# A second matrix product by Strassen's rule, in token blocks of 256

## The chip, the cores and the metric

The kernel runs on one core of a Trainium2 chip. Its engines work side by side, each through its own list of instructions in order: TensorE (matrix products; its weight loads are listed apart as PEld), VectorE (DVE), ScalarE (ACT), GpSimd (POOL), and SyncE (SP), which starts most of the DMA transfers. The metric is the device time of one execution in microseconds.

## What is computed

An attention block with a decaying state, followed by a feed-forward block. Cut to what matters:

```python
# q, k, v, f_logit: (4, 8, 768, 48)
f = 1 / (1 + exp(-f_logit))
for t in range(S):
    state = f[:, :, t, :, None] * state + einsum('bhd,bhe->bhde', k[:, :, t], v[:, :, t])
    y[:, :, t] = einsum('bhd,bhde->bhe', q[:, :, t], state)
x = y.transpose(0, 2, 1, 3).reshape(3072, 384)

h = x @ w_in                       # (3072, 384) @ (384, 2048)
g = h * erf(softplus(h))
out = g @ w_out                    # (3072, 2048) @ (2048, 384)
```

The kernel does the recurrence in 24 chunks of 128 tokens by matrix products, and the rest in blocks of several chunks. The weights come as 64-bit numbers and are turned into fp32 on the chip ("rounding"), in 16 pieces. The function of h is put together from a sigmoid and four tanh passes on ScalarE, and products on VectorE. All of it is fp32.

## The kernel before

A block has 3 chunks, so 384 tokens (TB), and there are 8 blocks. Each block passes through four stages: the chunk stages d, t, s and y, which end in the transposed x of the block; the first product (`hidden`); the activation; the second product (`project`). Stages of different blocks are interleaved on TensorE by a hand-made schedule: a loop goes through products one by one ("slots"), and at fixed slots it puts in chunk stages, steps of the activation and steps of the rounding.

The chunk stages, cut:

```python
def stage_d(g):
    ...
    nc.tensor.matmul(ps, lhsT=tri[:], rhs=lts[blk][:, j, :], start=True, stop=True)
    nc.scalar.activation(out=dp[:, :, 0:D], in_=ps..., func=AF.Exp, scale=-1.0)
    nc.scalar.activation(out=kd, in_=ps..., func=AF.Exp)
    ...
    nc.vector.tensor_tensor(out=qd[:, :, 0:D], in0=qns[g % NQ]..., in1=dp[:, :, 0:D], op=ALU.mult)
    (nc.vector if blk == 0 else nc.gpsimd).tensor_tensor(
        out=kd, in0=kns[g % NQ]..., in1=kd, op=ALU.mult)

def stage_t(g):          # four transposes of qd, four of kd, copied out as qT and kT
    ...
def stage_s(g):          # scores sc, A = sc * tri on VectorE, state: dS, Sn, Mbd (GpSimd)
    ...
def stage_y(g):          # y from A, v, qT and Mbd, copied to xT by ScalarE
    ...
```

The activation of one group of four tiles of d_ff (`h` is 128 x 1536). Each `yield` ends a step; a new group starts when the one before it has made LEAD = 5 steps:

```python
def activate(gr):
    h = gr["h"][:].rearrange("p j t -> p (j t)")
    e = epool.tile([P, FG * TB], FP32, name="e", tag="e")
    sigmoid(e, h)                          # ScalarE
    yield
    for i in range(n + 2):                 # n = 3
        if i < n:
            xs[i] = xpool.tile([P, FG * TB], FP32, name="x", tag="x")
            term(xs[i], h, i)              # ScalarE: tanh
        if i >= 2:
            times(e, xs.pop(i - 2), i - 2) # VectorE: e = (x + c) * e
        yield
    ...
    nc.scalar.activation(out=e[:], in_=e[:], func=AF.Tanh, scale=SERF_C)
    ...
    nc.vector.tensor_tensor(out=h, in0=h, in1=e[:], op=ALU.mult)
```

First and second product:

```python
def hidden(blk, gi):
    ...
    for u in range(FG // 2):
        hps = ps_moe.tile([P, 2, 512], FP32, name="hps", tag="moe")
        for j in range(2):
            ft = gi * FG + 2 * u + j
            for kt in range(n_k):                      # n_k = 3
                nc.tensor.matmul(
                    hps[:, j, 0:TB],
                    lhsT=w_in_sb[:, kt, ft * P : (ft + 1) * P],
                    rhs=xTs[blk][:, kt, :],
                    start=(kt == 0), stop=(kt == n_k - 1),
                )
                if j == 1 and kt == n_k - 1:
                    to = gr["h"][:, 2 * u : 2 * u + 2, :]
                    if blk < 2:
                        nc.scalar.copy(out=to, in_=hps[:, :, 0:TB])
                    else:
                        nc.vector.tensor_copy(out=to, in_=hps[:, :, 0:TB])
                    ...
                yield

def project(blk):
    ops = [ps_moe.tile([P, 2, 512], FP32, name="ops", tag="moe") ...]
    for gi in range(n_g):                              # n_g = 4
        for tt in range(CPB):                          # CPB = 3
            for j in range(FG):                        # FG = 4
                ft = gi * FG + j
                nc.tensor.matmul(
                    ops[tt // 2][:, tt % 2, 0:d_model],
                    lhsT=gr["h"][:, j, tt * P : (tt + 1) * P],
                    rhs=w_out_sb[:, ft, :],
                    start=(ft == 0), stop=(ft == n_ft - 1),
                )
                if ft == n_ft - 1 and tt == 1:
                    nc.scalar.copy(out=osb2[:], in_=ops[0][:, :, 0:d_model])
                    nc.sync.dma_start(...)             # 256 rows of the output
                if ft == n_ft - 1 and tt == 2:
                    nc.scalar.copy(out=osb1[:], in_=ops[1][:, 0, 0:d_model])
                    nc.sync.dma_start(...)             # 128 rows
                yield
```

The order of the loop: first product of block `it`, with the second product of block `it - 2` in its middle; chunk stages of block `it + 1`.

Of the kernel before, what the change touches and what calls it, by code (L numbers as in the profile page):

```python
# [65 lines left out]
P = 128  # L67
# [3 lines left out]
def kernel(  # L71
# [21 lines left out]
    CPB = 3  # L93
# [75 lines left out]
    epool = main.enter_context(tc.tile_pool(name="epool", bufs=3))  # L169
# [5 lines left out]
    NV, NQ, NG = 3, 3, 10  # L175
# [8 lines left out]
    Hgs = [fixed(f"Hg{i}", [P, FG, TB], pool=fix) for i in range(NG)]  # L184
    osb2 = fixed("osb2", [P, 2, d_model], pool=fix)
    osb1 = fixed("osb1", [P, d_model], pool=fix)
# [32 lines left out]
    HOMES = [("w", 0), ("w", 1), ("w", 2), ("w", 3), 4, 5, 6, 3] + [4, 5, 6, ("w", 2), ("w", 3), 7, 8, 9]  # L219
    ORDER = list(range(8)) + [8 + j for j in (0, 3, 1, 4, 2, 5, 6, 7)]  # L220

    def raw_home(i):
        if isinstance(HOMES[i], int):
            return Hgs[HOMES[i]][:].rearrange("p a t -> p (a t)")
        m = 2 * n_ft // n_pieces
        return w_out_sb[:, bass.ts(HOMES[i][1], m), :].rearrange("p a t -> p (a t)")
# [63 lines left out]

    xTs, As, qTs, kTs = {}, {}, {}, {}
# [35 lines left out]
    def stage_d(g):  # L327
        blk, j = divmod(g, CPB)
        if blk == 0:
            both = ps_moe.tile([P, 2, 512], FP32, name="ps_d0", tag="moe")  # L330
            ps, totals[g] = both[:, 0, 0:d_model], both[:, 1, 0:HP]
            busy.append(both[:, 1, P : 2 * P])
        else:
            ps = ps_at.tile([P, 512], FP32, name="ps_d", tag="at")[:, 0:d_model]
# [8 lines left out]
        if blk > 0:  # L343
            for a in range(HP):
                nc.sync.dma_start(
                    out=Tall[:, g, a : a + 1],
                    in_=dp[P - 1 : P, 2 * a : 2 * a + 2, :].rearrange("o r d -> o (r d)"),
                )
# [4 lines left out]
        (nc.vector if blk == 0 else nc.gpsimd).tensor_tensor(  # L353
# [3 lines left out]
    def stage_t(g):  # L357
        pss = []
        for src in (qd, kds[g % 2]):
            ps = ps_at.tile([P, HP, P], FP32, name="ps_t", tag="at")  # L360
            flat = src[:].rearrange("t (a r) d -> t a (r d)", r=2)
            for a in range(HP):
                nc.tensor.transpose(ps[:, a, :], flat[:, a, :], ident[:])  # L363
            pss.append(ps)
            if 0 < g < CPB and src is qd:
                keep_busy(3)
# [3 lines left out]
        if g < 3 * CPB:  # L370
# [58 lines left out]
    def stage_y(g):  # L429
# [4 lines left out]
        if blk == 0:  # L434
            keep_busy(3)
# [7 lines left out]
    def activate(gr):  # L443


        h = gr["h"][:].rearrange("p j t -> p (j t)")
# [23 lines left out]
    LEAD = len(SERF_KAB) + 2  # L470
# [12 lines left out]
    n_made = [0]  # L483

    def hidden(blk, gi):

        own = n_made[0] % NG
        gr = {"h": Hgs[own], "done": False}
        n_made[0] += 1
        groups[blk, gi] = gr  # L490
        for u in range(FG // 2):
            hps = ps_moe.tile([P, 2, 512], FP32, name="hps", tag="moe")
            for j in range(2):
                ft = gi * FG + 2 * u + j
                assert ft * n_pieces // n_ft in rounded
                for kt in range(n_k):
                    nc.tensor.matmul(  # L497
                        hps[:, j, 0:TB],
                        lhsT=w_in_sb[:, kt, ft * P : (ft + 1) * P],
                        rhs=xTs[blk][:, kt, :],  # L500
                        start=(kt == 0), stop=(kt == n_k - 1),
                    )
                    if j == 1 and kt == n_k - 1:
                        assert all(i in rounded for i, x in enumerate(HOMES) if x == own)
                        to = gr["h"][:, 2 * u : 2 * u + 2, :]
                        if blk < 2:
                            nc.scalar.copy(out=to, in_=hps[:, :, 0:TB])
                        else:
                            nc.vector.tensor_copy(out=to, in_=hps[:, :, 0:TB])  # L509
                        if u == FG // 2 - 1:  # L510
                            acts.append(activate(gr))
                    yield

    def project(blk):

        ops = [ps_moe.tile([P, 2, 512], FP32, name="ops", tag="moe")
               for _ in range(2 if blk < n_blocks - 1 else 1)]
        if blk == n_blocks - 1:

            ops.insert(0, ps_sc.tile([P, 2, 512], FP32, name="ops", tag="sc"))  # L520
        r = blk * TB
        for gi in range(n_g):
            gr = groups[blk, gi]
            for tt in range(CPB):
                for j in range(FG):
                    ft = gi * FG + j
                    assert n_pieces + ft * n_pieces // n_ft in rounded
                    while not gr["done"]:
                        act_step()
                    nc.tensor.matmul(  # L530
                        ops[tt // 2][:, tt % 2, 0:d_model],
# [4 lines left out]
                    if ft == n_ft - 1 and tt == 1:  # L536
                        nc.scalar.copy(out=osb2[:], in_=ops[0][:, :, 0:d_model])  # L537
                        nc.sync.dma_start(
                            out=out[r : r + 2 * P, :].rearrange("(t p) c -> p t c", p=P), in_=osb2[:]
                        )  # L540
                    if ft == n_ft - 1 and tt == 2:
                        nc.scalar.copy(out=osb1[:], in_=ops[1][:, 0, 0:d_model])
                        nc.sync.dma_start(out=out[r + 2 * P : r + TB, :], in_=osb1[:])
                    yield
# [4 lines left out]

    def slots(it):  # L550

        if it >= n_blocks:
            return project(it - 2)
        made = [hidden(it, gi) for gi in range(n_g)]
        return chain(*made) if it < 2 else chain(*made[:2], project(it - 2), *made[2:])

    n_h, n_o = n_ft * n_k, n_ft * CPB
    n_slots = [n_h] * 2 + [n_h + n_o] * (n_blocks - 2) + [n_o] * 2
# [17 lines left out]
    with tc.manual_schedule():  # L576
# [13 lines left out]
        for g in range(CPB, 2 * CPB):  # L590
            load_f(g)
# [62 lines left out]
        prepare(0, 2, 3)  # L654
# [15 lines left out]
        prepare(1, 0, CPB)  # L670
# [11 lines left out]
        def stages(blk):  # L682
            g0 = blk * CPB
            todo = []
            if blk == 1:
                todo = [(stage_d, g0), (stage_t, g0)]
            for g in range(g0, g0 + CPB):
# [9 lines left out]
        for it in range(n_blocks + 2):  # L697
            blk = it + 1
            if it + 2 < n_blocks:
                for j in range(CPB):  # L700
                    load_f((it + 2) * CPB + j)
            todo = deque(stages(blk) if blk < n_blocks else [])
            n = n_slots[it]
            at = [int(3 + (n - 13) / max(1, len(todo)) * i) for i in range(len(todo))]
            for s, _ in enumerate(slots(it)):
                due += 1 if it == 0 and s < 36 else 0.75
# [5 lines left out]
                if at and s == at[0]:  # L712
                    at.pop(0)
# [4 lines left out]
                if it + 2 < n_blocks and s == (16 if it < 2 else 30):  # L718
                    prepare(it + 2, 0, CPB)
                if it == 0:  # L720
                    step = s >= 16 and s % 8 == 4
                elif it == 1:
                    step = s % 8 == 4
                elif it == 2:
                    step = s % 3 == 1
                elif it < n_blocks:
                    step = s % 4 == 2
                else:
                    step = s % 3 == 2
                if step and not 66 <= s < 72:  # L730
                    act_step()
                if it == n_blocks - 1 and s in (5, 40):
# [216 lines left out]
```

## Time and profile before

| | |
|---|---|
| time, median of 3 | 647.7 us (647.5 to 647.84) |
| span of the profiled execution | 646.0 us |
| granted TensorE clock | 0.999 |
| ScalarE busy | 405.9 us (63%) |
| VectorE passes of the activation | 96 of 1806 ns, 32 of 1777 ns (mean) |
| GpSimd busy | 59.9 us (9%) |
| last product ends, last store is issued | 640.5 us, 641.1 us |

A line of the costliest groups reads: line of the kernel, engine, operation, what it writes and reads, shape, count, then busy time in us and the mean ns of one instruction, then the engine's idle time just before them and what ended most of it. A line of the timeline gives start and length in us of a run of equal instructions. A line of a table by stretch gives the stretch, its length, then busy us and count for TensorE, its weight loads, VectorE, ScalarE, GpSimd, then the granted clock, the DMA share and GB/s.

### The profile page before, as it was taken

What the parts mean: (1) busy time and instruction counts of PE and PEld (TensorE: products, weight loads), DVE (VectorE), ACT (ScalarE), POOL (GpSimd) and SP (SyncE); (2) the same over time, 40 slices, a digit from 0 to 9 for tenths busy, and PEclk for the clock granted to TensorE, in tenths of its full rate; (3) what the DMA queues carried; (4) which work ended last, traced back from release to release, by engine and by line L of the source; (5) the groups of instructions that cost most, each with busy time, mean ns of one, the idle gap of its engine ahead of it and who ended that gap; (6) DMA issues with size and microseconds to landing.
All of it is one profiled execution on the core that took longest, in us unless ns stands there. A gap on an engine that the chain in (4) does not pass through costs nothing.

```text
span 646.0 us, 9238 instructions
## 1 busy us (share of the span) xinstructions
PE 630.3 (98%) x3815; PEld 394.4 (61%) x3815; DVE 421.5 (65%) x408; ACT 405.9 (63%) x383; POOL 59.9 (9%) x61
## 2 busy tenths in 40 slices
PE   8999998999999999999999999999999999999996
PEld 7755665656666666666666566666666655555553
DVE  4798998899947765658654677447653686379100
ACT  5446768697888668656775757677564755276100
POOL 0112101111010000202210001100130000000000
PEclk9999999999999999999999999999999999999999
DMA  9995952310114120221202211020000000000101
GB/s 194 248 273 146 271 155 49 66 34 14 25 42 81 26 38 13 62 50 26 38 14 66 44 38 24 13 74 1 2 0 26 13 0 1 37 1 0 38 2 40
DMA packets 120688, 36.89 MB, mean 57 GB/s; under 512 B 112448, under 2 KB 115520, under 8 KB 120640
## 3 DMA queue, kind: packets, MB, share of 16 engines
q1 hardware_dynamic: 118560, 35.84, 24.1%
q10 hardware_dynamic: 2080, 0.39, 0.4%
q8 instruction: 32, 0.52, 0.3%
q14 instruction: 16, 0.13, 0.1%
HBM read 31.46 MB, written 4.72 MB: 56 GB/s over the span
## 4 chain that ended last, share of the span: by engine, by line
PE 89%; DVE 4%; ACT 3%; issue 2%; DMA 1%; SPq 0%; POOL 0%; ACTq 0%; POOLq 0%
PE ops L530 39%; PE hps L497 33%; PE y L145 5%; PE sc L381 3%; PE ps_t L363 3%; PE ps_d L335 2%; PE dS L409 1%; DVE e L159 1%; DVE w_out_sb L274 1%; PE ps_d L325 1%; PE busy L325 1%; DMA Tall<-dp 1%; PE ps_d L389 0%; DVE Hg L283 0%; ACT L299 0%
## 5 line engine op out<-in xcount | busy, mean ns | idle before, releaser
L497 PE MATMUL hps<-xT,w_in_sb 128*128 128x384 f32 x768 | 259.7, 489 | 1.1 <-ACT xT L438 0.6
L530 PE MATMUL ops<-w_out_sb,Hg 128*128 128x384 f32 x768 | 255.9, 489 | 0.0
L530 PEld LDWEIGHTS ops<-w_out_sb,Hg 128*128 128x128 f32 x768 | 143.8, 190 | 97.8 <-issue 2.2
L497 PEld LDWEIGHTS hps<-xT,w_in_sb 128*128 128x128 f32 x768 | 142.7, 190 | 96.0 <-issue 2.2
L159 DVE SCALAR_TENSOR_TENSOR e<-x,e 128x1536 f32<-128x1536 f32 x96 | 173.4, 1806 | 6.0 <-ACT x L154 3.0
L154 ACT ACTIVATE x<-Hg,serf_bias 128x1536 f32<-128x1536 f32 x96 | 147.5, 1569 | 18.8 <-DVE e L159 18.6
L509 DVE COPY Hg<-hps 128x768 f32<-128x768 f32 x48 | 45.9, 956 | 48.9 <-PE hps L497 48.7
L467 DVE TENSOR_TENSOR Hg<-Hg,e 128x1536 f32<-128x1536 f32 x32 | 56.9, 1777 | 11.7 <-ACT e L464 11.6
L353 POOL TENSOR_TENSOR kd<-kn,kd 128x384 f32<-128x384 f32 x21 | 33.0, 1570 | 329.4 <-issue 188.7
L349 DVE TENSOR_TENSOR qd<-qn,dp 128x384 f32<-128x384 f32 x24 | 14.2, 591 | 66.7 <-ACT dp L339 66.7
L151 ACT ACTIVATE e<-Hg,serf_bias 128x1536 f32<-128x1536 f32 x32 | 50.3, 1572 | 0.2
L464 ACT ACTIVATE e<-e 128x1536 f32<-128x1536 f32 x32 | 47.1, 1473 | 0.0
L537 ACT COPY osb<-ops 128x768 f32<-128x768 f32 x8 | 6.4, 796 | 60.4 <-PE ops L530 60.4
L438 ACT COPY xT<-y 128x384 f32<-128x384 f32 x24 | 11.5, 478 | 49.3 <-PE y L145 49.3
L395 DVE TENSOR_TENSOR A<-sc,tri 128x1024 f32<-128x1024 f32 x24 | 29.3, 1221 | 19.0 <-PE sc L381 18.7
L145 PE MATMUL y<-A,vt 128*32 128x128 f32 x768 | 35.2, 277 | 0.1
L339 ACT ACTIVATE dp<-ps_d 128x384 f32<-128x384 f32 x24 | 11.8, 491 | 36.9 <-PE ps_d L335 36.6
L145 PEld LDWEIGHTS y<-A,vt 128*32 128x32 f32 x768 | 27.4, 109 | 12.0 <-issue 6.8
L425 POOL TENSOR_TENSOR Mbd<-Sn,Tall 48x192 f32<-48x192 f32 x32 | 25.8, 807 | 91.0 <-DVE Sn L422 76.3
L369 ACT COPY qT<-ps_t 128x512 f32<-128x512 f32 x24 | 14.0, 582 | 28.7 <-PE ps_t L363 28.6
L381 PEld LDWEIGHTS sc<-qT,kT 48*128 48x128 f32 x384 | 23.3, 187 | 12.5 <-issue 11.3
L145 PE MATMUL y<-qT,Mbd 128*32 128x128 f32 x480 | 30.1, 273 | 0.0
(73 smaller groups left out, 426.2 us busy)
## 6 DMA issues: line engine op xcount, KB each, us to landing
lt<-in_f_logit_dram SPq DMA_DIRECT2D x24, 192.0 KB, 3.9
qn<-in_q_dram SPq DMA_DIRECT2D x24, 192.0 KB, 3.0
Hg<-in_moe_w_out_dram SPq DMA_DIRECT2D x6, 768.0 KB, 5.9
kn<-in_k_dram SPq DMA_DIRECT2D x23, 192.0 KB, 3.3
vt<-in_v_dram SPq DMA_DIRECT2D x23, 192.0 KB, 3.1
w_out_sb<-in_moe_w_in_dram SPq DMA_DIRECT2D x4, 768.0 KB, 6.5
Hg<-in_moe_w_in_dram SPq DMA_DIRECT2D x4, 768.0 KB, 7.8
out_dram<-osb SPq DMA_DIRECT2D x8, 384.0 KB, 2.5
```

Of the source, the lines that this page charges most:

```text
L145: nc.tensor.matmul(y[M * i : M * (i + 1), kt, :], lhsT=terms[n][0], rhs=terms[n][1], start=(n == 0), stop=(n == len(terms) - 1), skip_grou ...
L151: nc.scalar.activation(out=dst[:], in_=h, func=AF.Sigmoid, bias=serf_bias[:, 0:1])
L154: nc.scalar.activation(out=dst[:], in_=h, func=AF.Tanh, bias=serf_bias[:, 1 + i : 2 + i], scale=SERF_KAB[i][0])
L159: nc.vector.scalar_tensor_tensor(out=e[:], in0=x[:], scalar=SERF_KAB[i][2], in1=e[:], op0=ALU.add, op1=ALU.mult)
L353: (nc.vector if blk == 0 else nc.gpsimd).tensor_tensor(out=kd, in0=kns[g % NQ][:].rearrange("t (h d) -> t h d", d=D), in1=kd, op=ALU.mult)
L381: nc.tensor.matmul(sc[:, r, a, :], lhsT=kT[rows(r), a, :], rhs=qT[rows(r), a, :], start=True, stop=True,)
L395: nc.vector.tensor_tensor(out=A[:].rearrange("s r a t -> s (r a) t"), in0=sc[:].rearrange("s r a t -> s (r a) t"), in1=tri[:].unsqueeze(1) ...
L464: nc.scalar.activation(out=e[:], in_=e[:], func=AF.Tanh, scale=SERF_C)
L467: nc.vector.tensor_tensor(out=h, in0=h, in1=e[:], op=ALU.mult)
L497: nc.tensor.matmul(hps[:, j, 0:TB], lhsT=w_in_sb[:, kt, ft * P : (ft + 1) * P], rhs=xTs[blk][:, kt, :], start=(kt == 0), stop=(kt == n_k - 1),
L509: nc.vector.tensor_copy(out=to, in_=hps[:, :, 0:TB])
L530: nc.tensor.matmul(ops[tt // 2][:, tt % 2, 0:d_model], lhsT=gr["h"][:, j, tt * P : (tt + 1) * P], rhs=w_out_sb[:, ft, :], start=(ft == 0), ...
```

## The change

Blocks become 2 chunks, so 256 tokens, and there are 12 of them. For blocks 1 to 11 the second product follows Strassen's rule in Winograd's form. Per group of four d_ff tiles, the activated h is a 2 x 2 matrix of blocks (two halves of the tokens by two halves of the tiles), and w_out is one too (two halves of the tiles by two halves of the 384 columns). Seven products of blocks, each 192 columns wide, take the place of eight. They need sums of blocks of h (four per group and block), made by GpSimd from the activated h, and sums of blocks of w_out (four per group, made once, after block 0 has been projected in the plain way), and the seven results are combined by VectorE on the way out of PSUM. The aim is fewer columns through TensorE.

The diff, cut to its core:

```diff
-    CPB = 3
+    CPB = 2
@@
-    epool = main.enter_context(tc.tile_pool(name="epool", bufs=3))
+    epool = main.enter_context(tc.tile_pool(name="epool", bufs=2))
@@
-    Hgs = [fixed(f"Hg{i}", [P, FG, TB], pool=fix) for i in range(NG)]
+    Hring = fixed("Hg", [P, NG * FG * TB], pool=fix)          # NG = 12
+    wT = fixed("wT", [P, n_g, NT * FG // 2 * DH], pool=fix)   # sums of w_out; first holds block 0's h
+    NS, NA = 3, 3                                             # three sets of three sums of h
+    scratch = fixed("scratch", [P, S_WORDS + 7 * DH], pool=fix)
@@
-    LEAD = len(SERF_KAB) + 2
+    LEAD = len(SERF_KAB) + 3
@@ def hidden(blk, gi):
+        hps = ps_moe.tile([P, FG, TB], FP32, name="hps", tag="moe")
+        for j in range(FG):
+            ft = gi * FG + j
+            for kt in range(n_k):
+                nc.tensor.matmul(hps[:, j, :], lhsT=w_in_sb[:, kt, ft * P : (ft + 1) * P],
+                    rhs=xTs[blk][:, kt, :], start=(kt == 0), stop=(kt == n_k - 1))
+                if j == FG - 1 and kt == n_k - 1:
+                    if blk < 3:
+                        nc.scalar.copy(out=gr["h"], in_=hps[:])
+                    else:
+                        nc.vector.tensor_copy(out=gr["h"], in_=hps[:])
+                    acts.append(activate(gr))
+                yield
@@
+    def add(out, x, y, op=ALU.add):
+        nc.gpsimd.tensor_tensor(out=out, in0=x, in1=y, op=op)
+    def sum_w(gi):                       # four sums of 2 x 192 elements
+        add(t[:, 0], b12, b11, ALU.subtract)
+        yield
+        ...
+    def sum_h(gr):                       # four sums of 2 x 128 elements
+        while not gr["done"]:
+            act_step()
+        a11, a12, a21, a22 = blocks(gr["h"])
+        sums = next(sum_places)
+        add(sums[0], a21, a22)
+        yield
+        add(sums[1], sums[0], a11, ALU.subtract)
+        yield
+        add(sums[2], a12, sums[1], ALU.subtract)
+        yield
+        add(a21, a11, a21, ALU.subtract)
+        gr["sums"] = sums
@@ def project(blk):
+        place = {n: ops[i][:, j, k * DH : (k + 1) * DH] for n, (i, j, k) in {
+            1: (0, 0, 0), 2: (0, 1, 0), 6: (0, 1, 1), 5: (1, 0, 0), 7: (1, 0, 1), 3: (1, 1, 0), 4: (1, 1, 1),
+        }.items()}                       # (tile, bank, half)
+        def products(gis, ns):
+            ...
+                        nc.tensor.matmul(place[n], lhsT=x[:, j, :], rhs=y, ...)
+                        yield
+        yield from products((0, 1), (1, 2, 6))
+        yield from products((0,), (5, 7, 3, 4))
+        to_sum.appendleft(sum_h(groups[blk, 3]))
+        yield from products((1,), (5, 7, 3, 4))
+        yield from products((2, 3), (1,))
+        nc.scalar.copy(out=o[:, 3, :], in_=place[1])
+        yield from products((2, 3), (2, 6))
+        plus(o[:, 0:5:4, :], o[:, 3:4, :].broadcast_to((P, 2, DH)), pair(2))   # VectorE
+        yield from products((2, 3), (5, 7))
+        plus(o[:, 5:7, :], o[:, 4:5, :].broadcast_to((P, 2, DH)), pair(5))
+        plus(o[:, 3, :], o[:, 5, :], place[7])
+        yield from products((2, 3), (3, 4))
+        plus(o[:, 1:3, :], o[:, 5:7, :], pair(3))
+        store(blk)                       # 256 rows
@@ def slots(it):
+        if it == 0:
+            order = [h0[0], h0[1], h1[0], h0[2], h1[1], h0[3], h1[2], h1[3]]   # blocks 0 and 1
+        if it == 1:   # first product of block 2
+        if it == 2:   # first product of block 3, then block 0's plain second product
+        if it < n_blocks - 1:
+            return chain(project(it - 2), *hiddens(it + 1)), n_o + n_h
+        return chain(*[project(blk) for blk in range(n_blocks - 3, n_blocks)]), 3 * n_o
@@ in the loop over it and slot s
-                due += 1 if it == 0 and s < 36 else 0.75        # rounding steps per slot
+                due += 1 if it == 0 and s < 48 else 0.5
+                if it < 2:                                      # activation steps
+                    step = s % 12 == 6 and (it or s >= 24)
+                elif it == 2:
+                    step = s % 5 in (1, 3)
+                else:
+                    step = s % 4 == 2
@@
+                if it == 2:
+                    if s == n - 6:
+                        to_sum.extend(sum_h(groups[1, gi]) for gi in range(NS))
+                    sum_step()
+                elif it > 2:
+                    if s == n_o and it < n_blocks - 1:
+                        to_sum.extend(sum_h(groups[it - 1, gi]) for gi in range(NS))
+                    ...
+                    if s < n_o or s % 3 == 0 or it == n_blocks - 1:
+                        sum_step()
```

The chunk stages themselves are the same instructions; they now sit two chunks to a block, with the first three chunks still done ahead of the loop.

## The prediction, written before the changed kernel was run

> **What bounds the kernel now.** I read the busy shares first, then the slices, the costliest groups, and the timeline for the bound's unit price.
>
> ```profile
> PE 630.3 (98%) x3815; PEld 394.4 (61%) x3815; DVE 421.5 (65%) x408; ACT 405.9 (63%) x383; POOL 59.9 (9%) x61
> ...
> L497 PE MATMUL hps<-xT,w_in_sb 128*128 128x384 f32 x768 | 259.7, 489 | 1.1 <-ACT xT L438 0.6
> L530 PE MATMUL ops<-w_out_sb,Hg 128*128 128x384 f32 x768 | 255.9, 489 | 0.0
> ```
>
> TensorE is busy 98% of the span, and two groups hold most of it: first product (L497) and second product (L530). Each is 384 products of a 128x128 block (8 blocks of tokens x 16 tiles of d_ff x 3), and each fp32 product is two instructions. "Busy" proves no bound alone, because ends of matmuls are modelled, so I look for idle time by stretch. The columns are PE, PEld, DVE, ACT, POOL, granted clock, DMA:
>
> ```profile
> 32.40:145.00 112.60, 106.94 (x813) 67.32 (x814) 101.74 (x124) 80.69 (x95) 16.85 (x17) 1.00 0.59 142
> 145.00:500.00 355.00, 355.00 (x2161) 220.54 (x2160) 231.97 (x191) 247.59 (x218) 38.73 (x33) 1.00 0.16 33
> 500.00:640.50 140.50, 140.50 (x487) 82.73 (x485) 67.91 (x48) 61.47 (x45) 0.00 (x0) 1.00 0.03 13
> ```
>
> From 145 us to 640.5 us TensorE has no gap. From 32.4 us (first product) to 145 us it has 5.7 us of gaps, while VectorE, rounding the weights, is 90% busy. Before 32.4 us a chain of small steps fills the time; after 640.5 us come a copy and a store. So time is the sum of TensorE's work plus 32.4 us ahead and some 5.5 us behind, and any saved matmul time counts, if no other engine takes the bound.
>
> The unit price is the distance from one start to the next, not the 489 ns duration (they overlap). Timeline:
>
> ```profile
> 147.09 0.60 PE L363 MATMUL ps_t<-ident,kd 128*128 128x128 f32 x4
> ...
> 562.97 15.64 PE L497 MATMUL hps<-xT,w_in_sb 128*128 128x384 f32 x48
> ```
>
> For 384 columns: (15.64 - 0.49) / 47 = 322.3 ns. For 128 columns, every one with fresh 128x128 weights: (0.60 - 0.27) / 3 = 109 ns. The line through both: 0.833 ns a column plus 2.4 ns. So 256 columns cost 215.7 ns, and 192 columns 162.4 ns.
>
> [...] The trace shows 190 ns for a load, which is more than 162.4 ns, and would make the narrow products load-bound if loads ran end to end. They don't: transposes with 141 ns loads pass every 109 ns, and this group of plain fp32 products (weight loads of 192 ns median) took 0.94 us for six:
>
> ```profile
> 28.99 0.94 PE L325 MATMUL ps_d<-tri 128*128 128x128 f32 x6
> ```
>
> That is at most (0.94 - 0.28) / 5 = 132 ns each, below 162.4 ns.
>
> [...] Minimum/median/maximum ns of the groups:
>
> ```profile
> L353 POOL TENSOR_TENSOR kd<-kn,kd x21: 992/1372/2619, 36.9 to 471.8; 128x384 f32<-128x384 f32 x21
> ...
> L425 POOL TENSOR_TENSOR Mbd<-Sn,Tall x32: 498/504/1909, 23.4 to 479.2; 48x192 f32<-48x192 f32 x32
> ...
> L159 DVE SCALAR_TENSOR_TENSOR e<-x,e x96: 1736/1752/2560, 80.0 to 594.2; 128x1536 f32<-128x1536 f32 x96
> ```
>
> GpSimd's worst 2619 ns is close to its 997 ns plus most of a 1750 ns VectorE instruction. VectorE's worst 2560 ns is its 1750 ns plus most of a GpSimd one.
>
> [...] here (997 - 500) / 192 = 2.59 ns. I use the trace: a sum over 256 elements is 666 ns.
>
> **The change, part by part.**
>
> TensorE, first product. Twelve blocks x 48 products x 2 = 1152 instructions at 215.7 ns = 248.5 us, against 768 x 322.3 = 247.5 us. The smaller block costs 1.0 us, no more.
>
> TensorE, second product. Block 0 stays plain: 32 products x 2 x 322.3 ns = 20.6 us. The other eleven take 7 products x 8 (four groups, two tiles) = 56 products of 192 columns: 11 x 56 x 2 = 1232 instructions x 162.4 = 200.1 us. Together 220.7 us against 247.5 us: 26.8 us less, not the 31 us of one eighth, because block 0 keeps eight eighths and the fixed 2.4 ns is paid more often.
>
> Net -25.8 us on TensorE. The chunk work stays at 24 chunks: from 32.4 to 640.5 us are 608.1 us; minus 495.0 us of products and 5.7 us of gaps leaves 107.4 us for 21 chunks, 5.1 us each, unchanged.
>
> GpSimd gains 11 blocks x 16 sums x 0.666 = 117 us, and 16 sums of weights (384 elements) x 0.997 = 16 us. With its old work, 21 x 0.997 + 32 x 0.5 = 37 us unblocked, that is 170 us in 620 us. It's not a bound.
>
> VectorE. The passes of the activation become 192 of 1024 elements for 128 of 1536. A 1536 pass is 1750 ns[...]. So 192 x 1.217 = 234 us against 224 us. Copies out of PSUM: 36 x 1.224 = 44 us for 46 us. New: four combining additions a block, about 2.0 us, x 11 = 22 us (on ScalarE before, as copies). Waits for GpSimd: I guess 0.27 us per sum (half the sums find VectorE in a two-input pass, and then the next pass waits a whole 0.67 us more often than not) = 48 us. VectorE goes from 421 to about 500 us, 80% of the span. Per block in the steady part, VectorE has 16 passes 19.5 + copies 4.9 + additions 2 + two chunks 7.4 + waits 6 = 40 us, TensorE 18.2 + 20.7 + 10.2 = 49 us. TensorE remains the bound.
>
> ScalarE has fixed cost per pass, 48 groups for 32, but loses copies; per block some 34 us of 49.
>
> The start. Until the Strassen projections begin, TensorE has four first products (192 x 2 x 0.2157 = 82.8 us), block 0's projection 20.6 us and about seven chunks 36 us = 139 us. VectorE has 14.5 weight pieces of 4.6 us = 66, chunks 21, eight groups of activation 39 = 126 us, plus waits: 91%, as tight as now (90%). Local order is worse: weight steps come one per product, and a product is now 431 ns instead of 645 ns, with the first third of the loop waiting for pieces. Also block 1's activation is wanted right behind block 0's. I set gaps at 10 us for the present 5.7 us.
>
> The tail. The last addition is about 0.55 us like the last copy of 0.48 us; the last store doubles to 384 KB. +0.4 us.
>
> Sum: 32.4 + 248.5 + 220.7 + 107.4 + 10 + 5.9 = 624.9 us of span; the reported time lies 1.7 us above the span: 626.6 us. I say 626 us.
>
> **Rivals.**
>
> Weight loads bound the narrow products. For: 190 ns per load against 162 ns. Against: the 109 and 132 ns above. If loads ran end to end, 1232 x 28 ns = 34 us come back, some 660 us: no gain.
>
> VectorE and GpSimd lock each other out and VectorE becomes the bound. For: the stretched durations. If every sum delayed a pass, VectorE would have 34 + 16 x 0.67 + 4 = 49 us a block, level with TensorE; with lags at the hand-overs of PSUM buffers I would expect 640 to 650 us. Against: sums are spread over a long stretch, one every third product.
>
> The start starves: the bunched activation of block 1, or w_out pieces, stop TensorE for 20 us rather than 10: 636 us.
>
> TensorE waits for copies and additions within a projection. For: seven products share two buffers. Against: product 1 has a bank of its own, 2 with 6, 5 with 7, 3 with 4, and each bank is read when its products have ended, while TensorE writes the next.
>
> **Range and chances.** Nothing can save more than 26 us; with no more gaps than now it ends at 622 us, and with a start smoother than today's a few below. Upward the start (+10) and locking (+20) are open. Range 617 to 641 us. The 2% lines are 634.7 and 660.7 us: faster 0.78, same 0.19, slower 0.03.
>
> **What would show it.** Right: distances of 162 to 163 ns in the Strassen products and 216 ns in the first; TensorE without gaps after some 170 us; VectorE's median pass near 1.2 us with a long second peak up to 1.9 us; GpSimd near 200 us or more by waiting. Wrong: distances near 190 ns (loads); TensorE waiting for VectorE's copies at each block (locking); over 15 us of gaps before 180 us (start).

## The result: 698.3 us, slower, and the profile after

The changed kernel takes 698.31 us (697.49 to 701.82, 4 runs) against 647.77 us for the kernel before (4 runs): a ratio of 1.079, 95% interval 1.0751 to 1.0828. I had said 626 us, with a range of 617 to 641 us.

Busy time of the engines in the changed kernel (page of the profile), to be set against the 630.3 us and 98% of before:

```profile
PE 627.1 (90%) x4727; PEld 545.9 (78%) x4727; DVE 479.6 (69%) x508; ACT 429.0 (61%) x474; POOL 278.9 (40%) x253
...
PEclk9999999999898999899999899989999999999999
```

TensorE's busy time hardly fell, though 26 us of work were taken out of it, and its share fell to 90%. The second line shows slices in which its clock was not full: the mean granted clock is 0.964, against 0.999 before. The table by stretch (columns as before: TensorE, its loads, VectorE, ScalarE, GpSimd, clock, DMA, GB/s) shows where:

```profile
31.30:210.00 178.70, 160.48 (x1206) 127.67 (x1202) 141.34 (x160) 114.84 (x134) 50.49 (x44) 0.96 0.39 96
210.00:580.00 370.00, 333.25 (x2579) 295.30 (x2578) 248.27 (x237) 245.71 (x261) 164.15 (x147) 0.95 0.14 30
580.00:693.80 113.80, 106.42 (x595) 99.94 (x593) 70.61 (x66) 54.52 (x56) 60.17 (x52) 1.00 0.03 11
```

Before, TensorE had no gap after 145 us. Now it stands still for 36.8 us between 210 and 580 us, in the part that I had called steady. For whom it waits stands in the list of waits of TensorE (total us, times, longest us):

```profile
PE ops L650 <- DVE scratch L658: 26.4, 11, 5.8
PE ops L650 <- ACT scratch L666: 13.6, 11, 3.0
...
PE ops L605 <- DVE wT L493: 5.2, 1, 5.2
PE ops L650 <- DVE Hg L493: 4.1, 1, 4.1
```

L650 is the Strassen product, L666 the ScalarE copy of product 1, L658 the VectorE additions. Each of the two waits occurs 11 times, once per Strassen block: 40.0 us together. The timelines of TensorE and ScalarE in block 2 show the first of them:

```profile
270.19 1.46 PE L650 MATMUL ops<-w_out_sb,Hg 128*128 128x192 f32 x8
273.63 0.75 PE L650 MATMUL ops<-w_out_sb,Hg 128*128 128x192 f32 x2 [1.98 <-ACT scratch L666]
```

```profile
271.19 1.15 ACT L155 ACTIVATE e<-Hg,serf_bias 128x1024 f32<-128x1024 f32 x1
272.24 1.13 ACT L158 ACTIVATE x<-Hg,serf_bias 128x1024 f32<-128x1024 f32 x1
273.28 0.29 ACT L666 COPY scratch<-ops 128x192 f32<-128x192 f32 x1
```

The eight instructions of product 1 end; product 2 then waits 2 us for a copy of 0.29 us, which stands behind activation passes in ScalarE's list. And two instructions that span 0.49 us elsewhere span 0.75 us after the gap and 0.85 us just behind: the clock is halved there (0.50 granted from 274.0 to 276.8 us).

**The account.** In every kernel below I add up what TensorE's list holds: the time of the first product, the products at the distances of the prediction (469.2 us, or 496.0 us where all second products are plain), 107.4 us of chunk work, the gaps over 50 ns between matmuls after the first product, what the half clock took (half of each stretch granted 0.5), and what follows the last matmul.

| kernel | first product | products + chunks | gaps | half clock | behind | sum | span |
|---|---|---|---|---|---|---|---|
| as predicted | 32.4 | 576.6 | 10 | 0 | 5.9 | 624.9 | |
| changed kernel | 31.3 | 576.6 | 62.4 | 23.9 | 6.3 | 700.5 | 700.1 |
| e1_later | 31.5 | 576.6 | 34.4 | 10.2 | 7.1 | 659.8 | 661.9 |
| e2_banks | 30.5 | 576.6 | 26.5 | 8.6 | 6.6 | 648.8 | 649.5 |
| e4_plain256 | 31.8 | 603.4 | 20.8 | 3.4 | 6.6 | 666.0 | 666.9 |
| e18_vsum_all | 30.0 | 576.6 | 22.2 | 1.7 | 6.3 | 636.8 | 639.4 |

The sums close within 3 us. A part of the half clock lies inside gaps, though, and is counted twice: 6.5 us of the 23.9 us in the changed kernel, 1.3 us or less in the others. Without it the changed kernel's sum would be 694.0 us, 6 us short of its span. The price of the products was right, and the 75 us by which the span missed are about 52 us of gaps and, counted this way, 24 us of half clock.

### The profile page after: what moved, and what is told of

Read it like the earlier page. It is cut to its first block, busy times and chain, and to the rows that moved or that the text cites. A ratio compares the mean times of both kernels' runs of the same rounds, so it can differ in the third digit from the quotient of the medians.

```text
span 700.1 us, 11595 instructions
## 1 busy us (share of the span) xinstructions
PE 627.1 (90%) x4727; PEld 545.9 (78%) x4727; DVE 479.6 (69%) x508; ACT 429.0 (61%) x474; POOL 278.9 (40%) x253
## 4 chain that ended last, share of the span: by engine, by line
PE 64%; DVE 15%; ACT 10%; issue 4%; DMA 3%; POOL 2%; SPq 0%; ACTq 0%; DVEq 0%; POOLq 0%
PE hps L519 27%; PE ops L650 24%; PE y L149 4%; DVE e L163 3%; PE sc L407 3%; ACT x L158 2%; PE ps_d L361 2%; DVE scratch L658 2%; PE ps_t L389 1%; PE ops L605 1%; DVE A L421 1%; ACT e L155 1%; ACT L325 1%; DMA Hg<-in_moe_w_in_dram 1%; DVE Hg L308 1%
## 5 line engine op out<-in xcount | busy, mean ns | idle before, releaser
L519 PE MATMUL hps<-xT,w_in_sb 128*128 128x256 f32 x1152 | 262.8, 384 | 0.0
L519 PEld LDWEIGHTS hps<-xT,w_in_sb 128*128 128x128 f32 x1152 | 217.0, 191 | 33.6 <-issue 3.4
L163 DVE SCALAR_TENSOR_TENSOR e<-x,e 128x1024 f32<-128x1024 f32 x144 | 204.4, 1419 | 25.1 <-ACT x L158 22.3
L158 ACT ACTIVATE x<-Hg,serf_bias 128x1024 f32<-128x1024 f32 x132 | 146.8, 1136 | 0.1
L650 PE MATMUL ops<-w_out_sb,Hg 128*128 128x192 f32 x352 | 78.9, 339 | 17.6 <-ACT scratch L666 13.6
L650 PE MATMUL ops<-wT,Hg 128*128 128x192 f32 x352 | 88.6, 334 | 0.0
L650 PEld LDWEIGHTS ops<-w_out_sb,Hg 128*128 128x128 f32 x352 | 61.1, 194 | 24.9 <-ACT scratch L666 16.8
L650 PE MATMUL ops<-wT,scratch 128*128 128x192 f32 x320 | 77.3, 334 | 0.1
L493 DVE TENSOR_TENSOR Hg<-Hg,e 128x1024 f32<-128x1024 f32 x44 | 64.1, 1456 | 7.6 <-ACT e L490 7.3
L650 PEld LDWEIGHTS ops<-wT,Hg 128*128 128x128 f32 x352 | 63.5, 195 | 3.3 <-issue 2.0
L650 PE MATMUL ops<-w_out_sb,scratch 128*128 128x192 f32 x160 | 42.7, 350 | 25.4 <-DVE scratch L658 25.4
L658 DVE TENSOR_TENSOR scratch<-scratch,ops 128x384 f32<-128x384 f32 (+1 forms) x44 | 22.1, 502 | 56.6 <-PE ops L650 34.8
L650 PEld LDWEIGHTS ops<-wT,scratch 128*128 128x128 f32 x320 | 57.6, 195 | 0.6 <-POOL scratch L550 0.6
L650 PEld LDWEIGHTS ops<-w_out_sb,scratch 128*128 128x128 f32 x160 | 29.3, 203 | 28.3 <-DVE scratch L658 28.3
```

What stands on the lines that cost most here:

```text
L158: nc.scalar.activation(out=dst[:], in_=h, func=AF.Tanh, bias=serf_bias[:, 1 + i : 2 + i], scale=SERF_KAB[i][0])
L163: nc.vector.scalar_tensor_tensor(out=e[:], in0=x[:], scalar=SERF_KAB[i][2], in1=e[:], op0=ALU.add, op1=ALU.mult)
L519: nc.tensor.matmul(hps[:, j, :], lhsT=w_in_sb[:, kt, ft * P : (ft + 1) * P], rhs=xTs[blk][:, kt, :], start=(kt == 0), stop=(kt == n_k - 1),)
L650: nc.tensor.matmul(place[n], lhsT=x[:, j, :], rhs=y, start=(gi == 0 and j == 0 and n in first), stop=(gi == n_g - 1 and j == 1), skip_grou ...
L658: nc.vector.tensor_tensor(out=out, in0=x, in1=y, op=ALU.add)
```

## The experiments

Times are medians; "before" was run beside each and stayed at 647.4 to 647.9 us.

**The waits inside a projection.** e1_later only moves the copy and two additions behind the next products that write the same two-bank PSUM tile:

```diff
-        nc.scalar.copy(out=o[:, 3, :], in_=place[1])
         yield from products((2, 3), (2, 6))
+        nc.scalar.copy(out=o[:, 3, :], in_=place[1])
         plus(o[:, 0:5:4, :], ..., pair(2))
         yield from products((2, 3), (5, 7))
-        plus(o[:, 5:7, :], ..., pair(5))
-        plus(o[:, 3, :], o[:, 5, :], place[7])
         yield from products((2, 3), (3, 4))
+        plus(o[:, 5:7, :], ..., pair(5))
+        plus(o[:, 3, :], o[:, 5, :], place[7])
```

> Edit: the ScalarE copy of product 1 and the VectorE additions are put into the programs later, after the next products of the same two-bank PSUM tile instead of ahead of them; the same instructions otherwise. Theory (TensorE waits at two places in each Strassen projection, because the next product writes the same PSUM tile that a copy or addition reads, though another bank of it): the two waits go, about 40 us of TensorE's idle time after 210 us with them, and about 10 us of the slow clock that follows idle time: some 648 us. Rival (TensorE waits there for late sums, or VectorE is the bound through GpSimd's lock): the wait only moves to another place, 685 us or more.

Measured: 664.6 us. Both waits are gone, and 28 us of gaps with them. It didn't reach 648 us: the additions now come later, and the next first product waits for their PSUM tile (list of waits):

```profile
PE hps L519 <- DVE scratch L658: 6.8, 3, 4.8
```

e2_banks keeps the order and gives each bank a tile of its own (cut: the tiles of the first product and of the first chunks are parted in the same way, and so the copy of h becomes two copies of half the size):

```diff
-    ps_moe = ... tc.tile_pool(name="ps_moe", bufs=2, space=PSUM)
+    ps_moe = ... tc.tile_pool(name="ps_moe", bufs=4, space=PSUM)
-        ops = [ps_moe.tile([P, 2, 512], FP32, name="ops", tag="moe") for _ in range(2)]
+        ops = [ps_moe.tile([P, 512], FP32, name="ops", tag="moe") for _ in range(4)]
```

> Edit: order of the changed kernel kept; instead every PSUM tile of the two products is one bank (four buffers for two), so that copy and next product are never in one tile. 44 groups get two copies of 512 elements for one of 1024. Theory (it is the shared tile, not the bank, that makes TensorE wait): the same gain, 645 to 655 us. Rival (a copy or addition really has to come first, or the bank matters): stays within 10 us of 698 us.

Measured: 651.6 us, ratio to before 1.0079 (1.0056 to 1.0102), 46.7 us below the changed kernel. The same order of copies, additions and products runs without the waits. TensorE's timeline and the steady stretch of this kernel:

```profile
268.05 1.79 PE L653 MATMUL ops<-w_out_sb,Hg 128*128 128x192 f32 x10
```

```profile
240.00:560.00 320.00, 319.49 (x2523) 287.59 (x2523) 244.03 (x259) 234.97 (x250) 154.26 (x136) 1.00 0.15 31
```

Product 1's eight instructions and product 2's first two are one unbroken run, and TensorE is idle for 0.5 us in 320. So it was the shared tile that made TensorE wait, not the bank and not the data: the waits were written into the program for tiles. In this run ScalarE's copy of product 1 (at 271.15 us, 0.30 us long) runs while TensorE works on product 6 in the next bank (at 270.97 us, 0.49 us).

**The sums by GpSimd.** e3_nosums is e1_later, and e12_banks_nosums is e2_banks, without the 176 sums of h; the products read blocks of h in their place, so part of the computation is left out.

```diff
-        sums = next(sum_places)
-        add(sums[0], a21, a22)
-        ...
+        sums = [a11, a12, a22]
```

> Edit: e1_later without GpSimd's 176 sums of h; the products read blocks of h in place of the sums (this leaves out part of the computation). Theory (GpSimd's sums are hidden): within 5 us of e1_later. Rival[...]: at least 15 us below e1_later.

> Edit: e2_banks without GpSimd's 176 sums of h; products read blocks of h in place of the sums (this leaves out part of the computation). Theory (in the steady part the sums are hidden, only the first Strassen projections wait for them, 3.4 us and a stretch of half clock): 3 to 6 us below e2_banks, that is 646 to 649 us. Rival[...]: under 642 us.

Measured: 656.1 us, 8.4 us below e1_later, between theory and rival; and 645.1 us, 6.5 us below e2_banks, just outside the theory's window and short of the rival. (The rival in both is the prediction's: VectorE and GpSimd lock each other out and hold the kernel back.) The sums are not free, but they aren't the cause either. VectorE's busy time fell from 484.0 us in e2_banks to 455.8 us: 28 us for 176 sums, 0.16 us each.

**The blocks of 256 alone.** e4_plain256 has the new blocks and loop, and a plain second product everywhere, so no sums; its steady part has a step of the activation at every third product instead of every fourth (cut):

```diff
-            return chain(project(it - 2), *hiddens(it + 1)), n_o + n_h
+            return chain(project_first(it - 2), *hiddens(it + 1)), n_o + n_h
```

> Edit: blocks of 256 tokens and the new order of the loop alone; every second product is plain (32 products of 384 columns a block, no sums, no combining). TensorE's products then cost what they did before the change plus 1 us. Theory (the new start has about 17 us more gaps than before, and the plain projection has no inner waits): 660 to 670 us. Rival (the new start is harmless): 650 us. Rival (the block size itself is most of the loss): 690 us.

Measured: 667.6 us, ratio 1.0307 (1.0289 to 1.0325), inside the theory's window. The smaller blocks with the new start cost 20 us by themselves (16.8 of its 20.8 us of gaps lie before 225 us), and Strassen's rule with the tiles apart (e2_banks) wins back 16 us of the 26.8 us that its products save.

**The clock.** In the changed kernel the half clock comes in stretches of 3.4 or 6.8 us. Over all twenty traces (before, changed kernel, experiments) I set each gap of TensorE over 0.9 us, between first and last product, against the stretches of half clock:

| gap | number | with half clock during or right behind it |
|---|---|---|
| 0.9 to 1.9 us | 87 | 0 |
| 1.9 to 2.3 us | 57 | 24 |
| 2.3 to 4 us | 53 | 36 |
| over 4 us | 32 | 32 |

No stretch of half clock in that part came without such a gap. To part cause from company, e10_warm fills seven long waits of the changed kernel with products of no use, and e15_warm_start does so with the three longest waits of e2_banks:

```diff
+        warm(ops[1], 8 if blk in (2, 3, 5, 6) else 0)     # behind the copy of product 1
+        warm(ops[0], 20 if blk in (2, 4, 5) else 0)       # behind the additions to products 5 and 7
```

> Edit: the changed kernel, with products of no use (128x128 by 128 columns, into unused columns of PSUM) ahead of those waits that were long in its trace: 8 ahead of the first wait in blocks 2, 3, 5 and 6 (1.75 us each time), 20 ahead of the second in blocks 2, 4 and 5 (4.4 us). Theory (the halved clock is the answer to TensorE standing still for about 2 us or more): the five stretches of half clock between 270 and 465 us go, worth 9 us: 689 us, clock 0.98 or more. Rival (the clock has another cause, or is paid back inside the waits): 696 us or more.

> Edit: e2_banks, with products of no use ahead of the three long waits between 185 and 222 us (20, 16 and 12 of 128 columns; 4.4, 3.5 and 2.6 us). The waits stay as they are. Theory (half clock follows standing still): the 13.6 us of half clock there go, worth 5 to 7 us: 645 to 647 us. Rival: 651 us or more.

Measured: 693.3 us, 5.0 us below the changed kernel where I had expected 9; and 649.0 us, 2.6 us below e2_banks where 5 to 7 were expected. The same stretch of the changed kernel, and then of e10_warm:

```profile
270.00:465.00 195.00, 171.18 (x1275) 151.62 (x1275) 121.95 (x120) 129.92 (x138) 72.64 (x66) 0.93 0.16 33
```

```profile
270.00:465.00 195.00, 189.91 (x1510) 171.36 (x1509) 129.97 (x128) 133.57 (x142) 80.59 (x72) 1.00 0.19 39
```

The clock went from 0.93 to 1.00, with a known amount of useless work added. So standing still brought the half clock here. The 9 us were reckoned from the profiled execution of the changed kernel, which was the longest of its four (701.8 us, clock 0.964; two others took 697.5 and 697.6 us at 0.973): profile against profile the span fell by 8.9 us, from 700.1 to 691.2 us, and only the medians differ by 5.0 us. How much half clock an execution meets varies from one to the next. In e15_warm_start one stretch of 3.4 us stayed, behind a gap of 2.4 us at 216 us that the useless products had filled only in part.

**The start.** First the activation steps. e5_acts, e6_acts_sums and e7_late are e2_banks; e8_after_acts is the changed kernel:

```diff
-                if it < 2:
-                    step = s % 12 == 6 and (it or s >= 24)
+                if it == 0:
+                    step = s % 12 == 6 and s >= 24     # e7_late: False
+                elif it == 1:
+                    step = s % 4 == 2                  # e6, e7, e8: s % 3 == 1
                 elif it == 2:
-                    step = s % 5 in (1, 3)             # e5: as it was
+                    step = s % 2 == 1                  # e6, e7, e8
-                    if s == n - 6:                     # e5: as it was
+                    if s == n - 14:                    # e6, e7, e8
```

> Edit: e2_banks, with a step of the activation at every fourth product instead of every twelfth while block 2's first product runs (12 steps there for 4). Theory (between 180 and 225 us TensorE stands still because block 0's and block 1's activation was asked for too late[...]; VectorE was idle nearly half of 120 to 150 us): of the 12.7 us of gaps there some 9 go, with 3 us of slow clock: 640 us. Rival (VectorE simply has too much to do up to 225 us): gaps move, over 648 us.

> Edit: as e5_acts, with 16 steps in place of 12 there, a step at every second product in the next stretch, and the sums of block 1 asked for 14 products before the end of it, not 6. Theory: all 12.7 us of gaps between 180 and 225 us and the slow clock behind them go: 636 us. Rival as for e5_acts: over 645 us.

> Edit: as e6_acts_sums, and no steps of the activation at all while the first products of blocks 0 and 1 run (6 for VectorE's rounding to be freed of). Theory (from 32 to 90 us VectorE is the bound, 95% busy, and six steps are some 5 us of its work): 2 to 5 us less than e6_acts_sums. Rival (those gaps come from the order in which single chunk steps wait, not from VectorE's load): the same within 1 us.

> Edit: the changed kernel with the activation steps of e6_acts_sums and nothing else. Theory (the waits within a projection and the late start are two separate losses, and add): about 15 us below the changed kernel, 683 us. Rival (one hides the other): 695 us or more.

Measured: 655.2, 669.3, 665.5 and 719.6 us. All four are slower than what they started from, and the theory that the activation is merely asked for too late fell. (e7_late is 3.8 us below e6_acts_sums, as expected of it, but that is no gain.) ScalarE's timeline in e5_acts shows why:

```profile
113.18 0.84 ACT L342 ACTIVATE lt<-lt 128x768 f32<-128x768 f32 x1 [1.21 <-DVE lt L338]
114.06 0.84 ACT L343 ACTIVATE lt<-lt 128x768 f32<-128x768 f32 x1
114.91 1.28 ACT L158 ACT_TABLE_LOAD   x1
116.20 1.15 ACT L158 ACTIVATE x<-wT,serf_bias 128x1024 f32<-128x1024 f32 x1
117.26 1.05 ACT L529 COPY Hg<-hps 128x512 f32<-128x512 f32 x2
118.20 0.60 ACT L395 COPY qT<-ps_t 128x512 f32<-128x512 f32 x1
```

The step put in earlier (a table load and a pass, 2.4 us) stands ahead of the copy of qT, and TensorE's product y waited 4.2 us, up to 118.85 us, where in e2_banks it waited 1.8 us. ScalarE went through its list in order: the step moved forward pushed the chunk's own steps back. That isn't all: the two long waits for activation of e2_banks (5.3 and 4.0 us) are gone in e5_acts, as its theory had it, but TensorE now waits 6.4 us at 218 us for sums of h by GpSimd.

e9_block1_plain keeps block 1 plain too and spreads the sums of w_out behind it; e11_pace also rounds at three quarters of the pace:

```diff
+        if it == 3:
+            return chain(project_first(1), *hiddens(4)), n_ft * CPB + n_h
```

> Edit: e2_banks, with block 1's second product plain too; the sums of w_out then run in the stretch behind, at half the pace, and block 1 needs no sums of h. TensorE pays 2.4 us for it. Theory (the gaps from 185 to 225 us come from activation passes and sums[...] just where TensorE needs both): the 12.7 us of gaps there fall below 5 us, and 6 us of half-clock time go: 641 to 644 us. Rival (they come from the activation being asked for too late alone): 650 us or more.

> Edit: e9_block1_plain, with three quarters of a rounding step per product instead of one during the first 72 products. Theory (chunk steps from 32 to 90 us wait in VectorE's queue behind rounding steps, which come faster than VectorE does them): of some 10 us of gaps there half go: 4 to 6 us below e9_block1_plain. Rival (VectorE's load as such is the bound there): the same within 2 us.

Measured: 654.3 and 654.4 us. Neither helped: in e9_block1_plain two gaps of 4.1 us, at 212.5 and 239.6 us, took the place of the old ones (one for block 1's activation, one for VectorE's copy of h), and the pace of rounding changed which gap came where, not the sum much (26.7 and 25.3 us). But with the sums of w_out moved behind it, TensorE's wait for block 0's activation fell from 5.3 to 2.0 us.

e13_copies moves copies from ScalarE to VectorE, e14_copies_acts adds four activation steps to that, and e16_noround leaves VectorE's rounding of w_out away (part of the computation is left out):

```diff
-                        if blk < 3:          # copy of the first product by ScalarE
+                        if blk < 2:
-        if g < 9:                            # copy of kT by ScalarE
+        if g < 6:
```

> Edit: e2_banks, with the copies of block 2's first product and of kT of chunks 6 to 8 on VectorE instead of ScalarE (6 us of work). Theory (up to 225 us ScalarE's in-order list is what delays chunk steps and activation; VectorE is only half busy from 115 to 150 us): gaps up to 225 us fall from 28 us by 3 to 6 us: 645 to 649 us. Rival (VectorE's list is the one that delays): 652 us or more.

> Edit: as e13_copies, with 8 activation steps instead of 4 during block 2's first product. Theory (ScalarE's list): the room made lets the earlier steps pay, unlike in e5_acts: 3 us or more below e13_copies. Rival (more steps only push the chunk steps back): above e13_copies.

> Edit: e2_banks without VectorE's six rounding steps on each of the eight w_out pieces, 36 us of its work between 75 and 125 us (this leaves out part of the computation). Theory (gaps up to 80 us come from VectorE's rounding of w_in, those behind from ScalarE's list and late activation): only some 4 us of gaps at 89 to 126 us go: 645 to 649 us. Rival (VectorE's load decides the whole start): 15 us or more below e2_banks, under 637 us.

Measured: 650.9 us (0.7 us below e2_banks: not more than the runs scatter), 649.6 us (1.2 us below e13_copies, not the 3 expected) and 643.7 us (7.9 us below e2_banks, 1.3 us beyond the theory's window, and far from the rival). Without the rounding of w_out the gaps from 76 to 126 us vanish, those at 37 and 49 us and all behind 175 us stay. So VectorE's load makes the middle of the start's gaps, not all.

Behind 175 us the list of TensorE's waits in e2_banks, and then that in e14_copies_acts, name activation and sums:

```profile
PE ops L607 <- DVE wT L493: 5.3, 1, 5.3
PE ops L653 <- DVE Hg L493: 4.0, 1, 4.0
PE ops L653 <- POOL scratch L552: 3.4, 1, 3.4
```

```profile
PE ops L653 <- POOL scratch L552: 10.3, 3, 7.2
```

The timeline of GpSimd in e14_copies_acts shows sums of w_out (384 elements) back to back, and that of VectorE what runs beside them:

```profile
189.02 1.86 POOL L552 TENSOR_TENSOR wT<-w_out_sb,wT 128x384 f32<-128x384 f32 x1
190.84 2.00 POOL L552 TENSOR_TENSOR wT<-w_out_sb 128x384 f32<-128x384 f32 x1
192.81 0.99 POOL L552 TENSOR_TENSOR wT<-w_out_sb,wT 128x384 f32<-128x384 f32 x1
193.75 0.72 POOL L552 TENSOR_TENSOR scratch<-Hg 128x256 f32<-128x256 f32 x1
```

```profile
188.37 3.59 DVE L163 SCALAR_TENSOR_TENSOR e<-x,e 128x1024 f32<-128x1024 f32 x2 [0.31 <-ACT x L158]
197.45 0.56 DVE L375 TENSOR_TENSOR qd<-qn,dp 128x384 f32<-128x384 f32 x1 [5.49 <-ACT dp L365]
```

A sum takes 2.0 us while VectorE runs activation passes, and 0.99 us at 192.81 us, where VectorE is idle. The sums of h, for which the projection of block 1 waits, stand behind them. e17_vsum is e2_banks with these 16 sums on VectorE, e18_vsum_all is e14_copies_acts with the same edit:

```diff
-        add(t[:, 0], b12, b11, ALU.subtract)
+        add(t[:, 0], b12, b11, ALU.subtract, nc.vector)      # and the three others
```

> Edit: e2_banks, with the 16 sums of w_out on VectorE instead of GpSimd. Theory (from 172 to 220 us GpSimd works without a pause, and sums of w_out take 2.0 us instead of 1.0[...]; block 1's last sums come behind them): the wait for the last sums (3.4 us) goes, the waits for activation (5.3 and 4.0 us) shrink by half, with 7 us of half clock: 640 to 645 us. Rival (the waits for activation do not depend on the lock): only the 3.4 us and its half clock go, 647 us or more.

> Edit: e14_copies_acts, with the 16 sums of w_out on VectorE instead of GpSimd. Theory: there both late waits (2.6 and 7.2 us) are for sums alone, so most of 9.8 us and 5 us of half clock go: 636 to 640 us, below the kernel before. Rival: the waits move to VectorE, 645 us or more.

Measured: e17_vsum 648.8 us (647.2 to 651.9), a gain of 2.8 us, as the rival had it: the wait for the last sums went, but the wait for activation in block 0's projection grew from 5.3 to 6.8 us, now that VectorE has the sums to do as well. e18_vsum_all 642.9 us, 6.7 us below e14_copies_acts. That lies between theory and rival, and it is below the kernel before: ratio 0.9931, interval 0.9909 to 0.9953. Together the edits gained 8.7 us on e2_banks, 3.9 us more than the 2.0 and 2.8 us of each alone. With four to twelve executions of each kernel, which scatter over 3 to 5 us, this surplus is hardly clear of noise. The waits point the same way: with the activation earlier, GpSimd was the one for whom TensorE waited longest, and with the sums of w_out taken off it, it was not. The longest waits of TensorE in e18_vsum_all, none of them for a sum by GpSimd:

```profile
PE ps_t L389 <- DVE Sn L448: 8.8, 5, 2.8
PE ps_d L361 <- ACT lt L343: 3.1, 4, 1.2
PE ops L607 <- DVE wT L493: 3.0, 1, 3.0
```

What is left there are waits of chunk steps on VectorE and ScalarE. How the 22 us of gaps divide between VectorE's load and the order of its list stays open.

## Why the prediction was wrong

**Bound and prices: right.** TensorE's own work sets the time where it need not wait (319.49 us busy of the steady 320 in e2_banks). The distances between starts are 216 and 163 ns (medians) for 215.7 and 162.4 predicted, the weight loads of 190 ns don't bind, and the sum built from these prices closes for five kernels within 3 us (6 us in the changed kernel, if half clock inside gaps is not counted twice). VectorE's prices for 1024 elements, 1.217 us for a pass and 1.224 us for a copy, fit too: the product `A<-sc,tri` of that size took 1.224 us (median) in the kernel before, passes 1.239 and copies 1.225 us in the changed kernel. ScalarE's fixed cost per pass shows in its tanh passes: 1568 ns (median) for 1536 elements before, 1134 ns for 1024 in the changed kernel: 0.72 of the time for 0.67 of the elements.

**"TensorE waits for copies and additions within a projection": the step that failed.** I named it as a rival and dismissed it, because "each bank is read when its products have ended, while TensorE writes the next". That is true of the banks. But the tile was two banks, and the program made TensorE wait for the tile. It could be read in the code: `ops[0]` holds products 1, 2 and 6, and the copy of `place[1]` is written ahead of product 2. The trace of before even held two small cases of it. In the first chunks ScalarE reads one bank of a two-bank tile (`ps_d0`), and useless products, which read nothing but `tri`, write its other bank; in the list of waits of before:

```profile
PE ps_d L325 <- ACT kd L342: 1.9, 2, 1.0
```

The changed kernel has the same two waits; in e2_banks, where this tile is parted too, they are gone. Parting the tiles alone took 46.7 us off. My list of signs had named TensorE waiting at each block, but as a sign that GpSimd and VectorE lock each other out; leaving all sums of h away (e3, e12) shows that this was not the cause. The dismissed wait isn't the whole miss: e2_banks, without it, still spans 649.5 us against the predicted 624.9 us, through 16.5 us more of gaps than the 10 and 8.6 us of half clock.

**"I set gaps at 10 us": mis-sized.** The gaps up to 225 us were about 26 us in the changed kernel and in e2_banks alike. VectorE's rounding makes those from 76 to 126 us (e16_noround). Those behind 170 us, 12.7 us, are waits for activation and sums, which hold each other up and meet there (e9, e14, e17 and e18 together). The shares of VectorE's load that I compared, 91% and 90%, said nothing of the order in which in-order lists serve chunk steps.

**The half clock: missing from the sum.** A gap can be paid for again after it ends: 60 of the 110 gaps of 1.9 to 4 us brought half clock, and all 32 over 4 us. In the changed kernel its stretches are 3.4 or 6.8 us long at 0.5. Why one gap of about 2 us brought it and another did not was not shown. The kernel before had almost no gaps and lost nothing to it (1.00 granted from 32.4 to 640.5 us), so its trace was silent.

**GpSimd and VectorE locking each other out: they slow each other, harmlessly in the steady part.** In the changed kernel VectorE's passes `e<-x,e` took 1203 to 2034 ns, its copies out of PSUM of the same size 1211 to 1227 ns, and GpSimd's sums `scratch<-scratch,Hg` of 256 elements 724 to 1797 ns. That one shuts the other out for a whole instruction was not shown. I charged VectorE 0.27 us of waiting per sum, measured were 0.16 us (e12 against e2). VectorE was not the bound there: TensorE stood idle for 0.5 us in 320 in e2_banks. GpSimd's side I put too low: 666 ns for a sum of 256 elements, from a line through a group of 48 and one of 128 partitions, where the undisturbed sum took 0.72 us, and 170 to 200 us of busy time where it was 278.9 us. At one place, behind block 0's projection, it mattered: sums of w_out took 2.0 us beside VectorE's passes, against 0.99 us beside an idle VectorE (e14_copies_acts).

**Weight of the block size.** I charged smaller blocks with 1.0 us of TensorE's time, which is right for the products. e4_plain256 puts the whole at 20 us: about 15 us of gaps more than before, most of them before 225 us, and 3.4 us of half clock.

## What to carry to other kernels

When several accumulations share a PSUM tile, and one is read out while another goes on, ask what the program makes wait: if its waits are by tile, give each bank a tile, or put the reading behind the next writing (46.7 and 33.7 us here, e2_banks and e1_later). Reckon with half clock behind a TensorE gap of 2 us or more (92 of 142 gaps over 1.9 us had it here), and look for such gaps first when a change takes work away from an engine that was 98% busy. At a start where several in-order lists are near full, moving a step forward delays what stood there (in e5_acts product y waited 4.2 us instead of 1.8); try taking the work to another engine instead (6.7 us from e14_copies_acts to e18_vsum_all), and don't drop one of two remedies because it shows little before the other is in.

## What the runs showed that I had not expected

- TensorE's clock answered to gaps between 1.9 and 4 us in some cases and not in others (60 of 110); useless products in such gaps kept it at 1.00 between 270 and 465 us and gained 5.0 us in the medians (e10_warm).
- Two edits that gained 2.0 us (e14_copies_acts against e2_banks) and 2.8 us (e17_vsum) gained 8.7 us together (e18_vsum_all against e2_banks); the surplus is hardly clear of noise.
- An activation step moved to where VectorE was half idle made the kernel 3.6 us slower (e5_acts), and more of them 17.7 us (e6_acts_sums).
